# Reordering the first microseconds of a retention + ELU kernel: second chunk ahead of the first weight decode, powers later, one tile split by tokens

## The chip, the cores and the metric

The kernel runs on one core of one Trainium2 chip. The metric is the device time of that core in microseconds, over one launch. An engine name stands for the core's units: PE (matrix multiplication), DVE (vector), ACT (activation functions), POOL (general purpose), SP (which issues the transfers).

## What is computed

```python
# q, k, v: (4 batches, 8 heads, 768 positions, 64)
state = gamma * state + k_t^T v_t          # per head, 64 x 64
y_t   = (q_t . state) / sqrt(64)           # for every position t
x = y, heads side by side                  # (3072 tokens, 512)
h = x @ w_in                               # (512, 2048)
g = where(h > 0, h, exp(min(h, 0)) - 1)    # ELU
out = g @ w_out                            # (2048, 512)
```

`gamma` is one constant per head. All inputs and outputs are fp32; the weights arrive as 64-bit floats, of which the kernel itself makes fp32 numbers ("decode").

## The kernel before

**Tiling.** The 3072 tokens are handled in six blocks of 512; a block is four chunks of 128 tokens. One transfer of 1 MB (`load`, line 99) brings a chunk's q, k (turned) and k, v (plain). The retention is computed by chunk: powers of gamma are put on v (`scale_v`, line 275, which makes v'), a score matrix k q^T is masked (`score_products` 302, `mask_pair` 324), the state is k^T v' summed over half chunks of 64 tokens (`state_products` 332, `state_sum` 343), and the outputs are the masked part plus the part through the state (`within` 389, `across` 399), multiplied by powers of gamma out of a table `etab` (`powers_of`, line 246, four ACT exponentials per call). The result is the activations `xb`. The feed-forward part of the first block uses plain matrix products; the later blocks use Strassen's scheme on top of stored sums of weights. The change touches only the first block.

**Weights.** They come in 16 pieces of 1 MB (`load_piece`, line 126), of 64-bit words, into a ring of three staging buffers (`wraw`). `prepare` (line 147) issues the ACT part of a decode: two or three activations per part (lines 164, 166, 168). `decode` (line 180) is a generator with the DVE part: for each part a shift and mask (line 191, with a multiplication at line 190 ahead of it if `by_vector`), and an addition (line 194), after which the fp32 weights (`w_a`, `w_b`) are there. When the last part is done it also issues the load of the next piece. `take()` (line 1096) advances the generator by one step. Pieces 0, 1 and 2 are decoded in two halves of 512 columns.

**Order.** Nothing is scheduled automatically here. Each engine works through its instructions in the order in which the program text issues them, and lines 1106 to 1169 are a hand-written interleaving for the first 128 to 512 tokens. Generators hand out the work in steps:

- `outputs_of_first` (line 414) makes the activations of chunks 0 and 1 in two PSUM banks, `pb` and `pd`. Between the two groups of products into one bank stands a small DVE copy `seen` (line 426), for which the PE waits; line 433 writes `xb`.
- `plain_first` (line 489) makes 16 tiles of h, each of 128 rows of the result. The first five are begun on the first 256 tokens (`half[0]`, chunks 0 and 1), the rest of their tokens follows later. Tile 0 is further split: its first 128 tokens (chunk 0), a `yield`, then the next 128. Tiles 0 and 1 need the two halves of piece 0 (`w_a`), tiles 2 and 3 those of piece 1 (`w_b`), tile 4 the first half of piece 2. Tiles 0 to 4 are in the buffers pa, pa, pb, pd and hp.
- `unread` (line 1102) issues products of zeros whose result nobody reads.

In the order before, the first half of piece 0 is decoded on the DVE ahead of chunk 1's v' and mask, and the PE computes tile 0 on chunk 0 between chunk 1's scores and its k^T v'. The powers for tokens 256 to 767 (`between=` of `prepare`, line 1126) stand on the ACT between the two halves of piece 0. Chunks 2 and 3 are scaled by the POOL (line 281 as well, `scale_v(2)`, `scale_v(3)`); `scores(0, 1)` and `states(0, 1)` (lines 312 and 352) are their scores and states, `outputs(0, 1)` (line 364) their outputs, which read the later powers at line 384.

Of the kernel before, what the change touches and what calls it, by code (L numbers as in the profile page):

```python
# [18 lines left out]
def kernel(  # L19
# [36 lines left out]
    B, H, S, D, DM, DFF = dims  # L56
    NTOK = B * S
    C = P
    TB = 512
    TH = TB // 2  # L60
# [69 lines left out]
    def load_piece_parts(parts, behind=None):  # L130
        n = len(staged)
        if n < NPIECE:

            t = stage.tile([P, 1024, 2], U32, name="wraw", tag="stage")
            hold(t[:, :, 0].bitcast(FP32), behind)
            staged.append(t)
            for part in range(parts):
                if part:
                    yield
                c = slice(part * 1024 // parts, (part + 1) * 1024 // parts)  # L140
                d = slice(2 * c.start, 2 * c.stop)
                nc.sync.dma_start(t[:, c].rearrange("p c w -> p (c w)"), w_bits[n].bitcast(U32)[:, d])
# [1 line left out]

    def prepare(parts=1, by_vector=False, between=None):

        n = len(prepared)
        if n >= NPIECE:  # L150
            return
        t = staged[n]
        if n < 2 * NQ:
            dst = (w_a, w_b)[n % 2][n // 2].rearrange("p a b c d -> p (a b c d)")
        else:

            dst = w_s[n % NQ].rearrange("p a b c d -> p (a b c d)")[:, 0:1024]
        todo = []
        for part in range(parts):
            if part and between:  # L160
                between()
            c = slice(part * 1024 // parts, (part + 1) * 1024 // parts)
            lo, hi, flat = t[:, c, 0], t[:, c, 1], dst.bitcast(U32)[:, c]
            nc.scalar.activation(flat, lo, AF.Copy, scale=2.0**-29)
            top = dst.bitcast(F8).rearrange("p (c b) -> p c b", b=4)[:, c, 3]
            nc.scalar.activation(top, hi.bitcast(FP32), AF.Copy, scale=2.0**-120, saturate=False)
            if not by_vector:
                nc.scalar.activation(lo.bitcast(FP32), hi.bitcast(FP32), AF.Copy, scale=2.0**-112)
            todo.append((lo, flat, hi if by_vector else None))
        prepared.append((dst, todo))  # L170
# [9 lines left out]
    def decode(fine=False):  # L180

        n = len(decoded)
        if n >= NPIECE:
            return
        dst, todo = prepared[n]
        decoded.append(dst.rearrange("p (a b) -> p a b", a=2))
        vec = nc.vector
        for c, flat, hi in todo:
            if hi is not None:
                vec.tensor_scalar(c.bitcast(FP32), hi.bitcast(FP32), 2.0**-112, None, ALU.mult)  # L190
            vec.tensor_scalar(c, c, 3, 0x7FFFFFF8, ALU.logical_shift_left, ALU.bitwise_and)
            if fine:
                yield
            vec.tensor_tensor(out=flat, in0=c, in1=flat, op=ALU.add)
            yield
        load_piece()
        if n >= 2 * NQ:
            f = ORDER_F[n - 2 * NQ]
            nc.sync.dma_start(quarters(f)[:, used(f, 2, 8)], dst.rearrange("p (s c) -> p s c", c=P)[:, used(f, 2, 8)])
# [46 lines left out]
    def powers_of(tokens):  # L246
        for a in range(2):
            for u in range(2):
                nc.scalar.activation(etab[:, a, u, tokens], post[:, tokens], AF.Exp, scale=lny[:, a, u : u + 1])
# [4 lines left out]
    parts = load_piece_parts(2)  # L254
# [20 lines left out]
    def scale_v(m):  # L275
        if m >= NCHUNK:
            return
        i = chunks[m][1]
        qk, kv = raw[m]
        eng = nc.vector if m < 2 else nc.gpsimd  # L280
        eng.tensor_tensor(  # L281
            out=kv[:, 1], in0=kv[:, 1], in1=vf[:, i].unsqueeze(2).to_broadcast([C, H, D]), op=ALU.mult
        )
# [18 lines left out]
    def score_products(sc, tb, pp, x):  # L302
        qk = raw[tb * CPB + 2 * pp + x][0]
        for p in range(HP):
            for sub in range(2):
                for a in range(2):
                    nc.tensor.matmul(
                        sc[a][rows(sub), x, p, :], lhsT=qk[rows(a), 1, p, rows(sub)],
                        rhs=qk[rows(a), 0, p, rows(sub)], start=True, stop=True, skip_group_check=True,
                    )  # L310
# [32 lines left out]
    def state_sum(kvs, tb, pp, x, sub, copy=None):  # L343
        n = 4 * pp + 2 * x + sub
        if fresh(tb, n + 1):
            return
        if fresh(tb, n):
            (copy or nc.scalar.copy)(state(tb, n + 1), kvs[sub][:, x])
        else:
            nc.vector.tensor_tensor(out=state(tb, n + 1), in0=kvs[sub][:, x], in1=state(tb, n), op=ALU.add)  # L350
# [117 lines left out]
    def flush():  # L468
        while later:
            later.pop(0)()  # L470

    def elu(g, h, depth=1, then=None):


        r = epool.tile([P, 512], FP32, name="r", tag="r", bufs=3)
        e = r if len(h.shape) == 2 else r.rearrange("p (a c) -> p a c", c=P)
        nc.scalar.activation(e, h, AF.Relu, scale=-1.0)  # L477
        nc.scalar.activation(e, e, AF.Exp, scale=-1.0)  # L478

        def last():  # L480
            nc.vector.scalar_tensor_tensor(g, e, -1.0, h, ALU.add, ALU.max)  # L481
            if then:
                then()

        while len(later) >= depth:
            later.pop(0)()
        later.append(last)

    def plain_first():

        tiles = [(n, w, row, fi) for n in range(NQ) for w, row in ((w_a, 0), (w_b, 1)) for fi in range(2)]
        banks = []

        def part(k, columns):
            n, w, row, fi = tiles[k]
            for j in range(4):
                nc.tensor.matmul(
                    banks[k][:, columns], lhsT=w[n][:, fi, j // 2, j % 2, :], rhs=xb[:, j, columns],
                    start=(j == 0), stop=(j == 3), skip_group_check=True,
                )  # L500

        for k in range(5):
            hp = bank("aabd"[k]) if k < 4 else ps_r.tile([P, 2, TH], FP32, name="hp", tag="r")
            banks.append(hp.rearrange("p a b -> p (a b)"))
            if k == 0:
                part(0, slice(0, C))
                yield
                part(0, slice(C, 2 * C))
            else:
                part(k, half[0])  # L510
            if k:
                yield
        for k in range(5):
            part(k, half[1])
            n, w, row, fi = tiles[k]
            elu(g_plain[row * NF + 2 * n + fi], banks[k])
            yield
        for k, (n, w, row, fi) in enumerate(tiles[5:]):
            hp = bank("aabd"[k % 4]).rearrange("p a b -> p (a b)")
            for j in range(4):  # L520
                nc.tensor.matmul(  # L521
                    hp, lhsT=w[n][:, fi, j // 2, j % 2, :], rhs=xb[:, j, :], start=(j == 0), stop=(j == 3)
                )
            elu(g_plain[row * NF + 2 * n + fi], hp)
            yield
        flush()
# [158 lines left out]
    def bank(x):  # L685
        return ps_f.tile([P, 2, TH], FP32, name="p" + x, tag=x, bufs=2 if x == "a" else 1)
# [409 lines left out]
    def take(count=1):  # L1096
        for _ in range(count):
            next(piece, None)
# [3 lines left out]
    def unread(count, n):  # L1102
        for _ in range(count):
            nc.tensor.matmul(warm[:, 0:n], lhsT=blank[:, 0:P], rhs=blank[:, 0:n], start=True, stop=True, skip_group_check=True)
# [15 lines left out]
    y = outputs_of_first()  # L1120
    next(y)
    next(y)
    unread(1, TB)
    score_products(sc, 0, 0, 1)
    state_sum(kvs, 0, 0, 0, 1)
    prepare(2, between=lambda: powers_of(slice(2 * C, S)))
    piece = decode(True)
    take()
    take()
    scale_v(1)  # L1130
    mask_pair(sc, 1)
    inner = plain_first()
    next(inner)
    state_products(kvs, 0, 0, 1, range(2))
    state_sum(kvs, 0, 0, 1, 0)
    next(y)
    next(y)
    next(y)
    unread(1, TB)
    next(y, None)  # L1140
    take()
    take()
# [2 lines left out]
    scale_v(2)  # L1145
    scale_v(3)
    prepare(2, by_vector=True)
    next(inner)
    piece = decode()
    take()  # L1150
    take()
    next(inner)
    scores(0, 1)
    states(0, 1)
# [30 lines left out]
    for n, _ in enumerate(inner):  # L1185
# [8 lines left out]
        elif n == 10:  # L1194
            scores(1, 0)
            scores(1, 1)
            parts = sums_of_pieces(0)
# [21 lines left out]
    for n in second_of_first():  # L1219
        send_small()  # L1220
        if n == 0:
            run(inputs_of_first(4, [xslot(x) for x in range(3)]))
            parts = sums_of_pieces(2)
# [8 lines left out]
        elif n == 2:  # L1232
            next_piece()
            parts = sums_of_pieces(4)
# [5 lines left out]
        elif n == 4:  # L1240
            run(inputs_of_first(6, [hslot(), hslot(), xslot(0)]))
            decode_all()
            parts = sums_of_pieces(6)
# [85 lines left out]
    for tb in range(2, NTB):  # L1329
# [24 lines left out]
        tail, parts = iter(()), combine_x_parts()  # L1354
# [122 lines left out]
```

## Time and profile before

| what | value |
|---|---|
| median of 4 runs | 639.34 us (635.54, 640.03, 639.98, 638.70) |
| the profiled execution's own time | 635.54 us |
| its span, from the first to the last instruction | 633.7 us |
| PE busy | 626.1 us (99%) |
| DVE busy | 482.8 us (76%) |
| ACT busy | 253.4 us (40%) |
| POOL busy | 40.5 us (6%) |
| granted PE clock | 1.00 |

The profiled execution took 1.8 us more than its span, and is the fastest of the four. A busy PE counts every matmul from its start to a modelled end, so 99% doesn't mean that the PE has nothing left to gain, but its idle time is small. An fp32 matmul leaves two records in the trace: "x8" at line 497 is one tile's four matmuls. In the timeline, consecutive instructions of one kind are merged; the columns are the start, the time until the last one's end, the engine, the line, the operation, out<-in, the shapes, and in brackets the idle time before it with what ended it. Start times count from the start of the span. The addition at line 194 appears as CUSTOM_DVE_ANT_0.

### The profile page before, as it was taken

To read this page: it belongs to the slowest core of one execution; us is meant where nothing else is said; L and a number is where in the kernel's file an instruction comes from. 1 tells how busy PE (TensorE), PEld (TensorE's weight loads), DVE (VectorE), ACT (ScalarE), POOL (GpSimd) and SP (SyncE) were. 2 spreads that over 40 slices of the span, in tenths; PEclk is the share of its full clock that TensorE was granted. 3 is DMA by queue.
4 is the path that set the end of the run, shared out by engine and by line. 5 is a ranking of instruction groups with operands and counts; after the bars stand their busy time and mean duration, and the time that the engine had idled before them with its cause. 6 is when DMAs were issued, how large, how long until landed. Compare 5 with 4: busy or idle time off the path is not lost.

```text
span 633.7 us, 16149 instructions
## 1 busy us (share of the span) xinstructions
PE 626.1 (99%) x6680; PEld 560.5 (88%) x6680; DVE 482.8 (76%) x870; ACT 253.4 (40%) x472; POOL 40.5 (6%) x40
## 2 busy tenths in 40 slices
PE   8999999999999999999999999999999999999998
PEld 5764578888899999889999989999988999988997
DVE  5779979978879675589676588767489878558975
ACT  6599636014551113554112546111465311366311
POOL 1121000003600000200000100000110000000000
PEclk9999999999999999999999999999999999999999
DMA  8798868687477788504989701889820798700794
GB/s 337 269 399 315 252 202 234 189 250 258 176 230 241 242 258 274 220 2 139 287 259 314 285 2 54 258 284 287 302 100 5 219 300 259 216 20 2 229 310 159
DMA packets 75897, 136.85 MB, mean 216 GB/s; under 512 B 6320, under 2 KB 31792, under 8 KB 70704
## 3 DMA queue, kind: packets, MB, share of 16 engines
q1 hardware_dynamic: 75824, 135.82, 65.1%
q8 instruction: 53, 0.87, 0.5%
q14 instruction: 20, 0.16, 0.1%
HBM read 114.56 MB, written 21.23 MB: 214 GB/s over the span
## 4 chain that ended last, share of the span: by engine, by line
PE 93%; DVE 4%; DMA 1%; issue 1%; ACT 0%; SPq 0%; DVEq 0%
PE pa L953 20%; PE pa L911 10%; PE pd L953 10%; PE pb L953 5%; PE pa L865 5%; PE pb L911 4%; PE pa L521 3%; PE qa L911 3%; PE x L611 3%; PE pa L740 2%; PE pd L865 2%; PE qd L911 2%; PE pd L911 2%; PE pa L611 2%; PE y L394 2%; PE kv L338 2%
## 5 line engine op out<-in xcount | busy, mean ns | idle before, releaser
L961 ACT COPY ms<-pa 128x128 f32<-128x128 f32 x104 | 27.7, 267 | 147.0 <-PE pa L953 143.5
L953 PE MATMUL pa<-ts,wq 128*128 128x128 f32 x560 | 74.2, 275 | 0.0
L953 PE MATMUL pd<-ts,wq 128*128 128x128 f32 x552 | 73.6, 276 | 0.1
L953 PEld LDWEIGHTS pa<-ts,wq 128*128 128x128 f32 x560 | 68.5, 192 | 0.4
L953 PEld LDWEIGHTS pd<-ts,wq 128*128 128x128 f32 x552 | 67.1, 192 | 0.9 <-DVE res L965 0.5
L953 PE MATMUL pa<-gC,wq 128*128 128x128 f32 x480 | 64.6, 278 | 0.0
L478 ACT ACTIVATE r<-r 128x512 f32<-128x512 f32 x96 | 60.7, 632 | 3.0
L953 PEld LDWEIGHTS pa<-gC,wq 128*128 128x128 f32 x480 | 59.0, 192 | 1.3
L477 ACT ACTIVATE r<-gC 128x512 f32<-128x512 f32 x64 | 40.0, 625 | 33.0 <-DVE gC L919 33.0
L965 DVE TENSOR_TENSOR res<-pd,ms 128x128 f32<-128x128 f32 x68 | 19.5, 287 | 39.6 <-PE pd L953 38.4
L281 POOL TENSOR_TENSOR chunk<-chunk,vf 128x512 f32<-128x512 f32 x22 | 26.3, 1198 | 319.0 <-DMA chunk<-in_qkv_dram 235.1
L481 DVE SCALAR_TENSOR_TENSOR gC<-r,gC 128x512 f32<-128x512 f32 x64 | 45.3, 740 | 0.7 <-ACT r L478 0.7
L827 DVE TENSOR_TENSOR ts<-gC,ts 128x512 f32<-128x512 f32 x60 | 41.3, 688 | 1.0
L827 DVE TENSOR_TENSOR ts<-gC 128x512 f32<-128x512 f32 x60 | 41.0, 684 | 0.0
L953 PE MATMUL pb<-gC,wq 128*128 128x128 f32 x240 | 31.7, 275 | 0.0
L986 ACT COPY res<-pa 128x128 f32<-128x128 f32 x34 | 9.1, 267 | 55.0 <-PE pa L953 55.0
L953 PEld LDWEIGHTS pb<-gC,wq 128*128 128x128 f32 x240 | 29.2, 192 | 0.0
L690 ACT COPY m<-pa 128x512 f32<-128x512 f32 x24 | 14.0, 581 | 29.0 <-PE pa L911 13.2
L919 DVE TENSOR_TENSOR gC<-qa,gC 128x512 f32<-128x512 f32 x8 | 5.5, 692 | 25.1 <-PE qa L911 18.3
L911 PE MATMUL pa<-xt,w_s 128*128 128x256 f32 x96 | 23.0, 382 | 0.0
L911 PE MATMUL pa<-xt,w_b 128*128 128x256 f32 x96 | 23.0, 382 | 0.0
L965 DVE TENSOR_TENSOR res<-res 128x512 f32<-128x512 f32 (+1 forms) x31 | 20.6, 666 | 3.0 <-DVE res L965 0.5
(256 smaller groups left out, 1258.0 us busy)
## 6 DMA issues: line engine op xcount, KB each, us to landing
wq<-scratch_dram SPq DMA_DIRECT2D x277, 256.0 KB, 4.3
chunk<-in_qkv_dram SPq DMA_DIRECT2D x23, 1024.0 KB, 8.2
wraw<-in_w_dram SPq DMA_DIRECT2D x15, 1024.0 KB, 6.1
out_dram<-res SPq DMA_DIRECT2D x14, 256.0 KB, 3.8
scratch_dram<-gT SPq DMA_DIRECT2D x12, 256.0 KB, 4.1
scratch_dram<-m SPq DMA_DIRECT2D x12, 192.0 KB, 5.7
scratch_dram<-so SPq DMA_DIRECT2D x4, 512.0 KB, 4.8
scratch_dram<-wi SPq DMA_DIRECT2D x2, 1024.0 KB, 5.1
```

The source lines that it names most:

```text
L281: eng.tensor_tensor(out=kv[:, 1], in0=kv[:, 1], in1=vf[:, i].unsqueeze(2).to_broadcast([C, H, D]), op=ALU.mult)
L477: nc.scalar.activation(e, h, AF.Relu, scale=-1.0)
L478: nc.scalar.activation(e, e, AF.Exp, scale=-1.0)
L481: nc.vector.scalar_tensor_tensor(g, e, -1.0, h, ALU.add, ALU.max)
L521: nc.tensor.matmul(hp, lhsT=w[n][:, fi, j // 2, j % 2, :], rhs=xb[:, j, :], start=(j == 0), stop=(j == 3))
L611: nc.tensor.matmul(X[j][:, d, :], lhsT=w[j][:, d * P : d * P + P], rhs=x[j], start=(n == 0 and d == 0), stop=at_end, skip_group_check=True,)
L827: sub = lambda o, x, y: nc.vector.tensor_tensor(out=o, in0=x, in1=y, op=ALU.subtract)
L865: nc.tensor.matmul(ps[:, f, :], lhsT=lhs[f], rhs=xs[j][k], start=(begin and f == 0), stop=True, skip_group_check=True,)
L911: nc.tensor.matmul(ps[:, fi, :], lhsT=w[:, fi, j2, :], rhs=x[:, j2, :], start=(j in (1, 7) and fi == 0 and j2 == 0), stop=(j2 == 1), skip_ ...
L953: nc.tensor.matmul(ps, lhsT=w[:, f, :], rhs=ts[j][k][:, f, :], start=(begin and f == 0), stop=(f == 3), skip_group_check=True,)
L961: nc.scalar.copy(m, ps)
L965: nc.vector.tensor_tensor(out=o, in0=x, in1=y, op=ALU.add)
```

## The change

Only the order of instructions in the first block changes, with one tile split and two products of zeros shortened or dropped. The second call `unread(1, TB)` of this part shrinks to 256 columns and the third is dropped. The first piece's two DVE steps go behind chunk 1's v', mask and state sum, one on each side of the `seen` copies. Tile 0 on chunk 0 goes behind all of chunk 1's outputs on the PE. The four exponentials for the later tokens go behind the ACT part of piece 1. Tile 3 on the first 256 tokens is split into two halves of 128 tokens: one ahead of the scores of chunks 2 and 3, one behind their k^T v'. Queues of SP and POOL keep their order.

```diff
-    def prepare(parts=1, by_vector=False, between=None):
+    def prepare(parts=1, by_vector=False):
...
-            if part and between:
-                between()
...
+            elif k == 3:
+                part(k, slice(0, C))
+                yield
+                part(k, slice(C, 2 * C))
             else:
                 part(k, half[0])
...
     y = outputs_of_first()
     next(y)
     next(y)
-    unread(1, TB)
+    unread(1, TH)
     score_products(sc, 0, 0, 1)
     state_sum(kvs, 0, 0, 0, 1)
-    prepare(2, between=lambda: powers_of(slice(2 * C, S)))
+    prepare(2)
     piece = decode(True)
-    take()
-    take()
     scale_v(1)
     mask_pair(sc, 1)
-    inner = plain_first()
-    next(inner)
     state_products(kvs, 0, 0, 1, range(2))
     state_sum(kvs, 0, 0, 1, 0)
     next(y)
+    take()
     next(y)
+    take()
     next(y)
-    unread(1, TB)
+    inner = plain_first()
+    next(inner)
     next(y, None)
     take()
     take()
...
     scale_v(2)
     scale_v(3)
     prepare(2, by_vector=True)
+    powers_of(slice(2 * C, S))
     next(inner)
     piece = decode()
     take()
     take()
+    next(inner)
     next(inner)
     scores(0, 1)
     states(0, 1)
```

## Prediction, made before the changed kernel ran

> **What bounds the kernel now.** I read the page's busy rows first, then the PE's waits, then the timelines of PE, DVE, POOL and ACT from 8 to 32 us, where every edit lies, and last the chain of work that ended last.
>
> ```profile
> span 633.7 us, 16149 instructions
> PE 626.1 (99%) x6680; PEld 560.5 (88%) x6680; DVE 482.8 (76%) x870; ACT 253.4 (40%) x472; POOL 40.5 (6%) x40
> ```
>
> ```profile
> 10.38 0.69 PE L307 MATMUL sc<-chunk 64*64 64x64 f32 x32
> 11.32 1.13 PE L497 MATMUL pa<-xb,w_a 128*128 128x128 f32 x8 [0.25 <-DVE w_a L194]
> 12.38 0.69 PE L338 MATMUL kv<-chunk 64*64 64x64 f32 x32
> ...
> 14.69 1.12 PE L1104 MATMUL pa<-blank 128*128 128x512 f32 x2
> 15.65 3.11 PE L497 MATMUL pa<-xb,w_a 128*128 128x128 f32 x16
> 19.28 1.99 PE L497 MATMUL pb<-xb,w_b 128*128 128x256 f32 x8 [0.52 <-DVE w_b L194]
> 21.21 1.16 PE L307 MATMUL sc<-chunk 64*64 64x64 f32 x64
> ...
> 28.05 1.97 PE L497 MATMUL hp<-xb,w_a 128*128 128x256 f32 x8
> ```
>
> The PE is the bound: 633.7 - 626.1 = 7.6 us of it are idle in the whole span, and even with useless products counted as idle the stretch of the change has only a few us to give. After tile 4 (hp, 28.05) the chain that ended last runs through the PE without a gap to 46 us; DMA holds 1% of it in all, its first 4.9 us. So a shift of tile 4's start should be carried to the end: what I predict is that start.
>
> ```profile
> 10.48 0.69 DVE L194 CUSTOM_DVE_ANT_0 w_a<-wraw,w_a 128x1024 uint16<-128x1024 uint16 x1
> 11.09 0.69 DVE L281 TENSOR_TENSOR chunk<-chunk,vf 128x512 f32<-128x512 f32 x1
> 11.69 0.75 DVE L328 TENSOR_TENSOR chunk<-sc,cmask 128x256 f32<-128x256 f32 x2
> ...
> 17.92 1.31 DVE L194 CUSTOM_DVE_ANT_0 w_b<-wraw,w_b 128x1024 uint16<-128x1024 uint16 x1
> ...
> 20.17 1.35 DVE L194 CUSTOM_DVE_ANT_0 w_b<-wraw,w_b 128x1024 uint16<-128x1024 uint16 x1
> ```
>
> ```profile
> 17.51 1.17 POOL L281 TENSOR_TENSOR chunk<-chunk,vf 128x512 f32<-128x512 f32 x1 [2.39 <-DMA chunk<-in_qkv_dram]
> 19.93 1.04 POOL L281 TENSOR_TENSOR chunk<-chunk,vf 128x512 f32<-128x512 f32 x1 [1.25 <-DMA chunk<-in_qkv_dram]
> ```
>
> ```profile
> 9.69 2.55 ACT L249 ACTIVATE etab<-so,lny 128x512 f32<-128x512 f32 x4
> 12.42 0.69 ACT L164 ACTIVATE w_a<-wraw 128x512 uint32<-128x512 uint32 x1 [0.19 <-DMA wraw<-in_w_dram]
> ...
> 22.44 0.69 ACT L164 ACTIVATE w_a<-wraw 128x512 uint32<-128x512 uint32 x1 [4.67 <-DMA wraw<-in_w_dram]
> ```
>
> See three things. Chunk 1's scores start at 10.38, when its transfer is there, but its v' waits on the DVE behind the decode until 11.09. The same addition takes 0.69 us for `w_a` and 1.31 and 1.35 us for `w_b`, where POOL's scaling runs; both times it ends 0.55 us after POOL does (18.68 to 19.23, 20.97 to 21.52). And the ACT waits for transfers, on both sides of the powers.
>
> **The parts and their cost.**
>
> *Powers behind piece 1.* Four activations, 2.55 us, moved. Piece 0's second half still can't start before its transfer at 12.42 (0.19 us of wait today), so nothing is gained on the ACT. Piece 1's ACT part ends at 17.77 (16.98 + 0.79), the powers then run to 20.3, inside the 4.67 us wait before 22.44; their reader, the write of the second half of `xb`, comes at 28.12. Cost nothing, cover 2.1 us; were it gone, piece 2 and tile 4 would wait for it.
>
> *Products of zeros.* The halved one starts at 9.23 and is followed by the wait for chunk 1: no gain. The dropped one gives back 15.65 - 14.69 = 0.96 us, but only if `xb` and `w_a` are there earlier.
>
> *Chunk 1 first.* v' starts with its transfer at about 10.4 instead of 11.09 and ends at 11.05; the masks end at about 11.85 (12.44 before); k^T v' starts at 11.1, not 12.38, as tile 0's 0.9 us (the spacing of four 128-column matmuls in the later stages) no longer stands ahead of it. The state sum (13.11 before) runs 11.83 to 12.26, the PE's first products through it end at about 12.7. The moved shift (0.42 us) fits in between, 12.2 to 12.6, on the DVE ahead of `seen`, for which the PE waits: it costs nothing there by 0.1 us, and up to 0.1 if late. `seen` comes at 12.72 against 14.00: 1.28 us gained. The moved addition (0.69) follows, 12.9 to 13.6. Behind it on the DVE stand the two writes of `xb`: 13.5 to 14.25 (15.58 before); the PE's chunk 1 products are done by 13.5 and tile 0 waits for this addition till 13.65.
>
> *Tiles 0, 1, 2.* Tile 0's halves: 13.65 to 14.55 and, `xb` being there, to 15.45. Piece 0's second half on the DVE: shift at 14.5 (ACT ends at 14.44), addition to 15.65 (16.65 before). Tile 1: 15.7 to 17.45 (1.73 us, as four 256-column matmuls in the chain from 33 us on). Piece 1's first half: state sum 15.55, multiplication 15.9, shift 16.35, addition 16.9 to 17.6, just ahead of POOL's start at 17.51, hence 0.69 and not 1.31 us. Tile 2: 17.65 to 19.4, against 19.28: 1.63 us ahead.
>
> *Piece 1's second half against POOL.* [...] POOL's start is set by chunk 2's transfer and stays at about 17.5, [...] one of multiplication, shift and second addition is held for about 1 us: the addition ends at 20.2. By the rows without a block (0.42 + 0.43 + 0.69 and 0.2 of gaps) it would be 19.4; before it is 21.52. I take 20.2, as both collisions in the trace were lost by the DVE. So the block moves rather than goes.
>
> *Tile 3 split.* The same columns, four more matmuls and weight loads. Loads take 0.19 us and overlap; the later stages run 128-column matmuls in 0.9 us per four, against 1.73 / 2 = 0.87. Cost 0 to 0.1 us, taken as 0. Its first half waits for the addition: 20.25 to 21.15. The new wait is on the PE, and everything behind it (scores of chunks 2 and 3, their states) stands 0.06 us ahead of before. The second half saves 0.87 us behind the states: scores to 22.15, states to 23.15, tile 3's rest to 24.05, chunk 2 and 3's outputs from there (25.16 before).
>
> *To tile 4.* Outputs: 1.2 us of masked products, then those through the states, done by 25.75 (27.05). The DVE's masks and sums (22.35 to 25.4) are hardly earlier than before; its last sums, the shift and `seen` end at 26.0 without the 1.2 us of idle that they have before. DVE and PE now meet here. Second products through the states: 26.05 to 26.75, the addition for tile 4 done at about 26.7. Tile 4: 26.75 instead of 28.05.
>
> Sum: 1.28 us at `seen`, 1.63 at tile 2, 0.06 at the scores, 1.3 at tile 4: **1.3 us less**. Loads of pieces 3 and 4 are issued about 1 us earlier on SP, into queues that are full until 26 us: nothing. The profiled execution would go from 635.54 to 634.2. The other runs lie 3 to 4.5 us above it; taken off the median: 639.34 - 1.3 = **638.0 us**.
>
> **The rivals.**
>
> [...] (0.15). Its instructions are issued back to back, and POOL could wait until the second addition. Tile 3 then starts at 19.45, all behind it 0.8 us earlier: 2.1 us, 637.2. [...] Against: POOL was served each time before.
>
> *The DVE takes all* (0.18). If POOL's two instructions block twice (multiplication at 17.5, addition at 19.93), masks, sums and `seen` come 1 us later, tile 4 at 27.75: 0.3 us, 639.0; a second small delay, or `seen` behind a late shift, and it is no change. For it: the DVE has no idle left to absorb.
>
> *The clock falls* (0.12): slower. The products of zeros keep the PE busy. A 512-column one took 1.14 us at 1.5 us and 0.64 us at 9 to 15 us, though the granted clock shows 1.00 for both. [...] My longest new gap is 0.9 us (19.4 to 20.25)[...].
>
> **How the numbers follow.** The likeliest case has 0.55. A difference of 0.5% (3.2 us) is about what a measurement of this kernel can tell from no change, and no case reaches it: all waits and zeros of the stretch that can be recovered are under 3 us. What lies outside comes from the runs' scatter (635.5 to 640.0) [...]: faster 0.11, slower 0.07, within 0.82. The range goes from 635.3 (2.1 us gained, and the median halfway towards the fastest run) to 640.4 (the slow rival).
>
> **What would show it.** v' of chunk 1 on the DVE at 10.4; the first addition at 12.9; tile 0 at 13.65; `w_b` additions of about 0.7 us, first at 16.9, with a POOL or DVE instruction stretched by up to 1 us at 17.5; tile 3's first half at 20.25; tile 4 at 26.75, and the same shift in each later stage. I am wrong if tile 4 starts later than 27.7, if matmuls from 13.65 to 20 take twice their time, or if the 1.3 us are there at 28 us and gone at the end.

## The result, and the profile after

The change makes the kernel a little slower. The medians of all runs are 638.94 us after (636.67 to 641.98, 43 runs) and 637.01 us before (635.14 to 640.51, 64 runs; the median of the four runs shown ahead of the prediction was on the high side). The ratio is 1.0026, 95% interval 1.0017 to 1.0034: about 1.7 us (0.0026 x 637) more, where 1.3 us less had been forecast. The profiled execution after took 638.62 us, 2.0 us of it outside its span.

The page's first rows. PE busy falls by 0.9 us while the span grows by 2.9 us, so this is not more work but more idle time:

```profile
span 636.6 us, 16163 instructions
PE 625.2 (98%) x6686; PEld 560.6 (88%) x6686; DVE 481.1 (76%) x870; ACT 253.3 (40%) x472; POOL 40.4 (6%) x40
```

The PE's waits in the whole span (what it waited for, us in total, times, longest). The kernel before has no row with the releaser "issue", which is idle time for which the profile finds no semaphore:

```profile
PE y L407 <- issue: 1.3, 2, 0.9
PE pd L495 <- issue: 0.8, 1, 0.8
...
PE kv L336 <- issue: 0.5, 1, 0.5
PE pd L495 <- DVE w_b L192: 0.4, 1, 0.4
...
PE pb L955 <- issue: 0.2, 1, 0.2
```

The PE's timeline shows where they lie. Line numbers are now two lower around the retention, so L495, L305, L336, L407 answer to L497, L307, L338, L409:

```profile
10.41 0.69 PE L305 MATMUL sc<-chunk 64*64 64x64 f32 x32 [0.51 <-DMA chunk<-in_qkv_dram]
11.14 0.50 PE L336 MATMUL kv<-chunk 64*64 64x64 f32 x17
12.10 0.40 PE L336 MATMUL kv<-chunk 64*64 64x64 f32 x12 [0.46 <-issue]
...
14.46 3.77 PE L495 MATMUL pa<-xb,w_a 128*128 128x128 f32 x24 [0.23 <-ACT wraw L166]
18.23 1.97 PE L495 MATMUL pb<-xb,w_b 128*128 128x256 f32 x8
20.63 1.16 PE L495 MATMUL pd<-xb,w_b 128*128 128x128 f32 x8 [0.43 <-DVE w_b L192]
21.71 1.16 PE L305 MATMUL sc<-chunk 64*64 64x64 f32 x64
...
23.74 1.05 PE L495 MATMUL pd<-xb,w_b 128*128 128x128 f32 x7
25.61 0.27 PE L495 MATMUL pd<-xb,w_b 128*128 128x128 f32 x1 [0.82 <-issue]
...
27.77 0.69 PE L407 MATMUL y<-chunk 64*64 64x64 f32 x31 [0.33 <-DVE seen L376]
29.34 0.21 PE L407 MATMUL y<-chunk 64*64 64x64 f32 x1 [0.89 <-issue]
29.48 1.99 PE L495 MATMUL hp<-xb,w_a 128*128 128x256 f32 x8
```

Each stop falls in the middle of a run of equal matmuls: after 17 of 32 records, after 7 of 8, and after 31 of 32, just ahead of tile 4. The profile names no data for which the PE waits there. Tile 4 starts at 29.48 us, 1.43 us later than before and 2.73 us later than predicted.

### The profile page after: what moved, and what is told of

Its sections match the earlier page's. It is cut to its first block, busy times and chain, and to the rows that moved or that the text cites. A ratio compares the mean times of both kernels' runs of the same rounds, so it can differ in the third digit from the quotient of the medians.

```text
span 636.6 us, 16163 instructions
## 1 busy us (share of the span) xinstructions
PE 625.2 (98%) x6686; PEld 560.6 (88%) x6686; DVE 481.1 (76%) x870; ACT 253.3 (40%) x472; POOL 40.4 (6%) x40
## 4 chain that ended last, share of the span: by engine, by line
PE 87%; DVE 6%; DMA 2%; ACT 2%; issue 2%; SPq 0%; DVEq 0%
PE pa L955 20%; PE pa L913 10%; PE pd L955 10%; PE pb L955 5%; PE pa L867 5%; PE pb L913 4%; PE qa L913 3%; PE x L613 3%; PE pa L742 2%; PE pd L867 2%; PE qd L913 2%; PE pa L613 2%; PE pd L913 2%; PE y L392 2%; PE y L407 2%
## 5 line engine op out<-in xcount | busy, mean ns | idle before, releaser
L913 PE MATMUL pa<-xb,w_a 128*128 128x256 f32 x96 | 22.7, 379 | 0.0
```

The source lines that it names most:

```text
L913: nc.tensor.matmul(ps[:, fi, :], lhsT=w[:, fi, j2, :], rhs=x[:, j2, :], start=(j in (1, 7) and fi == 0 and j2 == 0), stop=(j2 == 1), skip_ ...
```

## What stops the PE

I counted the PE's records in the trace (weight loads, matmuls and its other instructions, in order of time): 13,614 before, 13,627 after. The instructions themselves come by DMA, in packets of 16 KB, as the page's part 3 shows (packets, MB, share of the engines):

```profile
q8 instruction: 53, 0.87, 0.5%
```

53 x 256 is 13,568, which fits 256 instructions to a packet. All the stops lie at records 193 + 256 k of the stream ("block ends" below): 449, 961 and 1217 early in the kernel after, 4801 and 6593 later. At these five stops the packet of the block that the PE needs starts 1.1 to 5.5 us after the PE has crossed the block end before it, takes about 1 us, and the PE goes on 1.36 to 1.45 us after the packet has ended. The 13 profiles of this document have 676 block ends: at none does the PE go on sooner than 1.18 us after its packet has ended, also where it doesn't stop. So at stops like these the PE goes on about 3.5 us (1.1 + 1 + 1.4) or more after it entered the block before; that is an estimate from these figures. Blocks of long matmuls last longer, and the packets are there in time: the 12 blocks of the kernel after that hold no product of the retention lasted 13.5 to 29.5 us, and the packet needed at the end of each had ended 8.0 us or more before the PE went on there. A block of the retention's 64x64 products need not last as long: 64 matmul records with their 64 loads take about 1 us (1.16 us at 21.71), at least half of the 256 records ahead of each stop are of that kind, and those blocks lasted 2.6 to 7.1 us.

With the change the block end 449 falls into chunk 1's k^T v', which now starts at 11.14, ahead of the block; before, it started at 12.38, when the block was there. The end 1217 lay 11 instructions inside tile 4, where it left a gap of 0.2 us; now it lies in the outputs just ahead of tile 4. In the kernel before, one stop is above 0.25 us (0.27 us at 77 us); after, there are five, 3.99 us in sum, of which 2.87 us (0.67 + 1.10 + 1.10) come before tile 4. The last two are 2.20 of the 2.73 us by which tile 4 misses the prediction; 0.38 more had been lost when tile 3's first half started (20.63 instead of 20.25). The stop at 449 doesn't add in full, as part of it went into the wait for `w_b` there.

The tile's split adds 16 instructions (four more matmuls and four loads, each of which leaves two records in fp32); the dropped product of zeros takes 4 away, and there is one more semaphore: +13.

Theory A, **instruction blocks**: the loss is stops at block ends, made by the count of instructions ahead of the dense stretches and by their earlier start. Theory B, **the moves**: the new order itself costs, for example by the powers behind piece 1, DVE against POOL, or later weight loads; the count doesn't matter. A third, the **clock** (the prediction's rival), is taken up where the traces show it.

## The experiments

Ratios are to the kernel before, with 95% intervals (6 executions each for the two with +48, 10 to 22 for the others, 43 for `after`). "Stops" are those over 0.25 us at block ends in the one profiled execution, counted as above; a wait of 0.96 us at end 705 of `after_p48` is left out, as its packet had been there for 3.4 us and the PE waited for `w_b`. The products of zeros in the opening loop (`range(28)`) serve as a dial: four of them are 16 instructions, their result is read by nobody, and no computed work is changed.

| kernel | edit | ratio | stops, sum in us | tile 4 at, us |
|---|---|---|---|---|
| before | | 1 | 1, 0.27 | 28.05 |
| after | the change | 1.0026 [1.0017, 1.0034] | 5, 3.99 | 29.48 |
| after_m16 | after, 28 to 24 | 1.0033 [1.0018, 1.0048] | 2, 2.55 | 30.05 |
| before_p16 | before, 28 to 32 | 1.0024 [1.0003, 1.0044] | 6, 3.85 | 29.72 |
| after_p48 | after, 28 to 41, one `unread` less | 1.0072 [1.0052, 1.0092] | 2, 2.98 | 30.10 |
| before_p48 | before, the same | 1.0080 [1.0057, 1.0102] | 3, 3.75 | 29.98 |
| after_nosplit | after, tile 3 whole | 0.9995 [0.9977, 1.0014] | 0, 0.00 | 29.36 |
| after_nosplit_p16 | the same, 28 to 32 | 1.0021 [1.0013, 1.0030] | 3, 2.40 | 28.88 |
| before_split | before, tile 3 split | 1.0038 [1.0024, 1.0052] | 5, 3.39 | 30.22 |
| after_powers_back | after, powers as before | 1.0025 [1.0013, 1.0038] | 5, 3.65 | 29.23 |
| after_nosplit_again | as after_nosplit | 0.9993 [0.9977, 1.0009] | 2, 1.33 | 27.41 |
| before_m16 | before, 28 to 24 | 1.0028 [1.0014, 1.0043] | 3, 2.18 | 28.47 |
| after_nosplit_m8 | after_nosplit, 28 to 26 | 1.0014 [1.0000, 1.0028] | 3, 1.55 | 27.39 |

The stops are not all that a profile lost. In four of the profiles the granted clock falls to 0.50 for 3.41 us: `after_nosplit` (from 12.31 us), `after_m16` (15.10), `after_p48` (12.52 and 227.56) and `before_p48` (229.22). Each of these five stretches begins 0.4 to 1.8 us after the end of an idle time of 1.45 to 1.90 us, at a stop or in a wait for chunk 1. (Idle means that neither a matmul nor a weight load is on record.) The other idle times between the first scores and the last matmul are at most 1.13 us long, and none is followed by such a stretch.

### The count alone, up and down

The kernel before with four more products (`before_p16`); `after_m16` has 24 in the same line of the kernel after.

```diff
-    for n in range(28):
+    for n in range(32):
```

> The kernel before, with 32 instead of 28 small products of zeros at the start: 16 more PE instructions, nothing else moved. Theory (PE instruction blocks): the block's end, 11 instructions into tile 4 today, falls 4 instructions ahead of it, so tile 4 waits for the fetch: it starts at 29.0 to 29.2 instead of 28.05 us and the kernel is about 1.0 us slower (ratio 1.0016), without any part of the change. Rivals (DVE and POOL, clock): at most the 0.2 us that the four products take, and those are in a wait for the first transfer: ratio 1.0000.

> The changed kernel with 24 instead of 28 small products of zeros at the start: 16 fewer PE instructions ahead of everything, nothing else moved. Theory (PE instruction blocks): in the changed kernel the PE stops at instruction 193 + 256k of its own stream (449, 961, 1217) until 1.4 us after the instruction transfer of that block has ended; the last such stop (1.1 us) stands right before tile 4. With 16 fewer instructions the block's end falls 14 instructions into tile 4, whose matmuls are slow enough to hide the fetch: tile 4 starts at about 28.3 instead of 29.48 us, and the time is 1.2 us below the changed kernel, about 0.5 us above the kernel before. Rival ([...] the multiplication held 1.27 us at 18 us): no vector instruction moves, so no change, tile 4 at 29.4, 1.7 us above the kernel before. Rival (clock, fewer zeros): if anything slower.

`before_p16` moves nothing and adds four tiny products, and is slower by 0.24%. The PE's timeline has the stops of the kernel after at the same places:

```profile
25.74 0.70 PE L497 MATMUL pd<-xb,w_b 128*128 128x256 f32 x2 [0.43 <-issue]
...
28.32 0.69 PE L409 MATMUL y<-chunk 64*64 64x64 f32 x30 [0.33 <-DVE seen L378]
29.47 0.33 PE L409 MATMUL y<-chunk 64*64 64x64 f32 x2 [0.45 <-issue]
29.72 1.56 PE L497 MATMUL hp<-xb,w_a 128*128 128x256 f32 x6
```

Two stops before tile 4 (0.81 and 0.67 us) and four later ones make the 3.85 us of the table. (In this profile chunk 1's scores also started 0.7 us later than before, at 11.08; see "Open".) B can't explain that. But `after_m16` didn't win the time back. The stop at 1217 is gone, as expected, and a longer one has come at 449, where the packet ran 10.95 to 11.91 us (9.79 to 10.68 in the kernel after):

```profile
11.20 0.62 PE L336 MATMUL kv<-chunk 64*64 64x64 f32 x25
13.27 0.28 PE L336 MATMUL kv<-chunk 64*64 64x64 f32 x4 [1.45 <-issue]
...
15.52 5.18 PE L495 MATMUL pa<-xb,w_a 128*128 128x128 f32 x24 [0.17 <-DVE w_a L192]
```

The last row is tiles 0 and 1, which took 3.77 us in the kernel after: from 15.10 to 18.51 us the clock was at half. So the count sets where the ends lie, but not simply how much is lost: a slightly later end (the one at 193 was crossed at 7.18 us instead of 6.92) gave a packet 1.2 us later, and behind the long stop the clock fell, which cost 1.41 us more. Without these 1.41 us tile 4 would have stood at about 28.6 us (30.05 - 1.41, an estimate), near the 28.3 expected. The clock isn't the whole of the miss in the times, though: the 10 executions of `after_m16` at a clock of 0.999 or more still have a median of 637.9 us, against 636.3 for those of the kernel before.

### Forty-eight more

```diff
-    for n in range(28):
+    for n in range(41):
...
     mask_pair(sc, 0)
-    unread(1, TH)
```

> The changed kernel with 41 instead of 28 small products of zeros at the start and without the 256-column one behind chunk 0's scores: 48 more PE instructions ahead of chunk 0's products of v. Theory (PE instruction blocks): block ends fall into chunk 1's scores (reached later than the fetch lands), into tile 2, into chunk 3's states (23.4 us) and into the last products through the states; only the last one still stops the PE, by under 1 us, at about 27.1. Tile 4 at 27.1 to 27.6 us, about 2 us below the changed kernel and 0.5 to 0.9 us below the kernel before, which is what the prediction had counted on. Rivals (DVE and POOL, clock): as the changed kernel, 1.7 us above the kernel before, tile 4 at 29.4.

> The kernel before with the same 48 PE instructions more at the start: a control, which says whether such instructions are of use by themselves. Theory (PE instruction blocks): only one stop of 0.2 us at 25.3 us is there to be removed, tile 4 at 27.8 to 28.1 us, ratio 0.9995 to 1.0005. Rival (the zeros help by the clock): the gain of the other kernel with 48 would show here as well, 2 us.

Missed in both. I had worked out the early ends only. In both kernels the end 4801 now falls into the outputs at 227 us, with the same long stop; the first line is of the kernel before with this edit, the second of the kernel after with it:

```profile
227.60 0.34 PE L409 MATMUL y<-chunk 64*64 64x64 f32 x7 [1.84 <-issue]
```

```profile
227.15 0.46 PE L407 MATMUL y<-chunk 64*64 64x64 f32 x14 [1.85 <-issue]
```

That two orders share it speaks for A: the place follows the count. The stop at 4801 (2.07 us after, 2.06 before) and the later tile 4 (2.05 and 1.93 us) make about 4 of the 4.6 and 5.1 us lost. Right behind this stop the clock is at half for 3.41 us in both; the clock row of the page of `before_p48`, 16 us to a digit, shows it as the one 8:

```profile
PEclk9999999999999989999999999999999999999999
```

Chunk 1's scores also started 0.9 to 1.0 us later here (11.35 and 11.30); that part is not settled, see "Open".

### The split alone, and the change without it

```diff
-            elif k == 3:
-                part(k, slice(0, C))
-                yield
-                part(k, slice(C, 2 * C))
...
-    next(inner)
     scores(0, 1)
```

`before_split` adds these lines to the kernel before, and moves nothing else; `after_nosplit` takes them out of the kernel after.

> The kernel before with tile 3 split by tokens as in the change, and nothing else: 16 more PE instructions ahead of tile 4. Theory (PE instruction blocks): as with 16 products' worth of instructions at the start, a stop of about 1 us ahead of tile 4, which starts at 29 to 29.7 instead of 28.05 us, plus the wait of tile 3's first half for its weights at 21.5 us; 1 to 2 us slower (ratio 1.0015 to 1.003). Rival (the split is free and saves PE time ahead of the outputs): 0 to 0.9 us faster.

> The changed kernel with tile 3 left whole, behind the states of chunks 2 and 3, as before. Theory (PE instruction blocks): 16 fewer instructions stand ahead of tile 4, so the block's end falls into tile 4 instead of right ahead of it, and the scores, no longer behind tile 3's wait for its weights, start when chunk 3 has landed (20.2 to 20.5 us instead of 21.7), which also starts the next fetches earlier. Tile 4 at 26.8 to 27.6 us instead of 29.48; 1.5 to 2.5 us below the changed kernel, 0 to 1 us below the kernel before (ratio 0.998 to 1.000). The stop at instruction 449 (chunk 1's states, 12 us) stays. Rival (the loss comes from the moves in the first 16 us, not from the split): as the changed kernel, ratio 1.0026. Rival (DVE held by POOL): the second half of piece 1 is late as before, but nothing waits for it ahead of 22 us, so it can't be told from the first.

> The same with 32 instead of 28 small products of zeros: 16 more PE instructions, so the block's end stands two instructions ahead of tile 4 again, as in the changed kernel. Theory (PE instruction blocks): a stop right ahead of tile 4, of about 1 us: tile 4 at 28 to 28.5 us, 0.8 to 1.3 us slower than without these products. Rival (only the order of PE, DVE and ACT matters): the same time as without them.

The split alone costs 0.38%; the rest of the change, without the split, shows no cost (0.9995, and 0.9993 when it was run again). `after_nosplit_p16` has no split but as many PE records as the kernel after (13,627), and is slow again, 1.0021. So most of the split's price is its instructions, not its order. In the first profile of `after_nosplit` chunk 1's scores started only at 11.89 us and the clock was at half behind that wait, so its tile 4 at 29.36 says little.

> The changed kernel without the split of tile 3 once more: for a narrower interval, and for a profile with another landing of chunk 1's transfer, which came 1.5 us late in the first one. Theory (PE instruction blocks): ratio 0.998 to 1.000 as before; if chunk 1 lands at 10.4 us, tile 4 at 26.8 to 27.6 us, with a stop of about 0.6 us at instruction 449 and none at 961 and 1217. If the moves of the first 16 us were themselves the loss, tile 4 would stand at 28.05 us or later with chunk 1 at 10.4.

The second profile of the change without the split, in which chunk 1 landed as early as in the kernel after, gives the account. The PE's timeline:

```profile
18.22 1.97 PE L495 MATMUL pb<-xb,w_b 128*128 128x256 f32 x8
20.11 1.16 PE L305 MATMUL sc<-chunk 64*64 64x64 f32 x64
...
24.88 1.05 PE L392 MATMUL y<-chunk 64*64 64x64 f32 x57 [0.48 <-issue]
...
26.72 0.69 PE L407 MATMUL y<-chunk 64*64 64x64 f32 x32 [0.33 <-DVE seen L376]
27.41 1.97 PE L495 MATMUL hp<-xb,w_a 128*128 128x256 f32 x8
```

Tile 2 starts at the same time as in the kernel after (18.22, 18.23), tile 4 2.07 us earlier. Without the split the scores follow tile 2 at once, at 20.11. With it, tile 3's first half stands there and waits for `w_b` until 20.63: 0.52 us. The remaining ends cost 1.10 + 1.10 with the split and 0.69 (at 961) without: 1.51 us. 0.52 + 1.51 = 2.03 of the 2.07 us. The times agree, within wide intervals: 1.0026 - 0.9993 is 0.0033, 2.1 us. The multiplication beside POOL's scaling takes as long in this kernel, 1.27 us, and `w_b` comes at the same time (20.55 and 20.57 us); so DVE against POOL shows no cost by itself, only through the wait that the split puts ahead of the scores.

### The powers, and two more counts

> The changed kernel with the four exponentials back between the two halves of piece 0, where they stood before. All theories: they stand in a wait of the ACT in either place, so no change from the changed kernel, ratio to before 1.002 to 1.003. If they had been the cause, the ratio would go to 1.000.

```diff
-    prepare(2)
+    prepare(2, between=lambda: powers_of(slice(2 * C, S)))
...
-    powers_of(slice(2 * C, S))
```

1.0025 against 1.0026: the move of the powers shows no cost, as predicted. B has lost its first candidate.

Two more counts: the kernel before with 24 products (`before_m16`), and `after_nosplit` with 26 in the same line (`after_nosplit_m8`).

```diff
-    for n in range(28):
+    for n in range(24):
```

> The kernel before with 24 instead of 28 small products of zeros: 16 fewer PE instructions, the counterpart of 16 more. Theory (PE instruction blocks): the block's end moves from tile 4 into the tile behind it, so no stop ahead of tile 4; at most one of 0.6 us at instruction 449, if its fetch comes late: ratio 0.9995 to 1.001, against 1.0024 with 16 more. Rival (any change in the number of these products disturbs the start): slower by as much as with 16 more.

> The changed kernel without the split and with 26 instead of 28 small products of zeros: a try at a version that beats both, as the first block's end is crossed a little later, [...]. Theory (PE instruction blocks): no stop ahead of tile 4, ratio 0.997 to 1.000. Other theories: as without the split.

`before_m16` was expected at no change and is slower, 1.0028. Tile 4 is only 0.4 us later, 0.57 of stop being at 449; a longer stop stands at 1729, in the second block of tokens:

```profile
65.25 0.85 PE L338 MATMUL kv<-chunk 64*64 64x64 f32 x37
67.12 0.39 PE L338 MATMUL kv<-chunk 64*64 64x64 f32 x6 [1.01 <-issue]
```

I had again thought of the early ends only; the stops of 2.18 us in sum do fit the 1.8 us. `after_nosplit_m8` lies between `after_nosplit` and the slow ones, with 1.55 us of stops. Over the table, every kernel with over 2 us of stops is slower than before, the one with 1.55 has an interval that just touches no change, and the two that aren't slower have 0 and 1.33. It isn't a straight line: the two with +48 lose more than their stops, and `after_m16` with 2.55 loses as much as `after` with 3.99. These three are kernels in whose profiles the clock fell behind a stop.

## Why the prediction was wrong, step by step

**Right.** Chunk 1's v' started at 10.39 (10.4 predicted). The powers hid where they should, on the ACT with 2.54 us of wait left behind them:

```profile
17.60 2.54 ACT L247 ACTIVATE etab<-so,lny 128x512 f32<-128x512 f32 x4
22.67 0.69 ACT L162 ACTIVATE w_a<-wraw 128x512 uint32<-128x512 uint32 x1 [2.54 <-DMA wraw<-in_w_dram]
```

Beside POOL's first scaling it is now another DVE instruction that takes longer, as the step on piece 1's second half had it. DVE and POOL timelines:

```profile
17.39 0.69 DVE L192 CUSTOM_DVE_ANT_0 w_b<-wraw,w_b 128x1024 uint16<-128x1024 uint16 x1
18.00 1.27 DVE L188 TENSOR_SCALAR wraw<-wraw 128x512 f32<-128x512 f32 x1
...
19.87 0.70 DVE L192 CUSTOM_DVE_ANT_0 w_b<-wraw,w_b 128x1024 uint16<-128x1024 uint16 x1
```

```profile
17.91 1.07 POOL L279 TENSOR_TENSOR chunk<-chunk,vf 128x512 f32<-128x512 f32 x1 [2.86 <-DMA chunk<-in_qkv_dram]
```

The first addition now takes 0.69 us; the multiplication behind it, 0.42 us elsewhere, takes 1.27 and ends 0.29 us after POOL (18.98). In the profile before, no multiplication ran beside POOL's scaling, so that a multiplication takes longer there shows only here. The second addition ended at 20.57 instead of 20.2; POOL's scaling ended 0.3 us later than before.

**The rival of the clock.** Tile 2's four 256-column matmuls take 1.97 us, against 1.99 before, and the granted clock stayed at 1.00 in the profile after: the rival of a falling clock isn't what made tile 4 late there. It isn't out for the times. A clock below 0.999 over the whole execution stands in 60 of the 174 executions on record of the eight kernels with the change (9 of 44 of `after`), and in 18 of the 195 recorded with a clock of those without it. For `after` that is a small part: leaving the nine out lowers its median by 0.3 us. The idle times that were followed by half the clock were 1.45 to 1.90 us long; the longest new gap of the prediction was 0.9 us.

**Wrong, first: "Tile 3 split. ... Cost 0 to 0.1 us, taken as 0."** This is the term that turned the sign. I priced four more matmuls by their time on the array, which came out nearly as priced (1.08 and 0.97 us for the halves, 1.93 for the whole tile before), and put nothing for their 16 instructions, which move every later block end. What they cost: 1.51 us at tile 4 in the profiles, and 0.0027 of the time (1.0021 against 0.9994, the mean of the two), or 1.7 us, by the count alone.

**Wrong, second: the new wait was compared with the wrong kernel.** I noted that everything behind tile 3's first half stands "0.06 us ahead of before". Against the same change without the split it stood behind a wait of 0.52 us in which the scores could have run, and my own numbers had that wait in them (tile 2 to 19.4, the half from 20.25).

**Wrong, third: "k^T v' starts at 11.1" and the state sum at 11.83.** It started at 11.14, but stopped after its 17th record for 0.67 us; the sum came at 12.58, `seen` at 13.47 instead of 12.72. The 1.28 us of gain there became 0.53.

The upper end of the range, 640.4 for the slow rival, was my estimate and rests on no trace.

**What became of the rest.** Later in the kernel the ends 4801 and 6593 cost 0.52 and 0.60 us. In the profiled execution 0.7 us more were lost at about 72 us, where the outputs of the second block wait for a DVE sum, behind a weight piece that landed late (the ACT waited 1.30 us for it at 55 us, before not at all). The kernel's loads there are the same. Six of the eight profiles with the change have this wait of the PE (0.3 to 0.6 us), and one of the five without, so it may belong to the change; no run tests it. Without the split the change should still have given up to 1.3 us. It gave 0.64 at tile 4 and 1.0 us of span in one profile, and 0.3 to 0.5 us in the times, with intervals that include no change. Part of the rest is the clock: among executions at 0.999 or more its medians are 635.8 and 635.7 us, against 636.4 and 636.5 of the kernel before, 0.6 and 0.8 us less. Its two stops, 0.64 and 0.69 us, are the likeliest place of the remainder, which is not shown; no count that was tried removes both and adds none.

**Open.** Chunk 1's transfer lands at 10.3 to 10.6 us in most profiles and at 11.1 to 11.9 in five. In four of the five the first block end was crossed about 1 us earlier, so that an instruction packet was fetched ahead of part of that chunk; in the fifth, `after_nosplit`, it wasn't. That a packet delays the chunk is therefore only a guess. It doesn't set the verdicts alone: `after_m16`, `before_split` and `before_m16` are slow, and their profiles have an early chunk 1. Why the clock fell more often with the change is open too: the shortened product of zeros stood ahead of the wait for chunk 1, and the stops are new idle time, but no run separates them.

## What to carry to other kernels

An instruction can have a price even where its execution is hidden (here 0.0027 of the time for 16 of them): on an engine that is never idle, count the instructions, find where the ends of the instruction blocks fall, and see whether a stretch of short instructions stands there. A stop marked "issue" in the middle of a run of equal matmuls (0.43 to 1.85 us here) was the sign of it. For a gain of some tenths of a per cent, first move the count alone in the kernel before (a few useless products, at no other change) and see how much the time scatters with it; here that was 0.2 to 0.3% for four products (0.8% with 48 instructions more), more than the whole expected gain. Price each part of a change against the change without that part, not only against the kernel before. And where a profile has a long pause (here 1.45 us or more), read the clock behind it as well.

## What the runs showed of the hardware

The arrival of instructions stopped the PE. In the kernel after, each of the 52 packets ended 1.36 us or more before the PE went on into the block that the count gives it, and began while an earlier block ran. At 36 of the 52 ends the PE shows no gap above 0.05 us; at the five stops 150 to 255 of the 256 records ahead are of 64x64 products, and the gaps are 0.52 to 1.10 us, 3.99 us in sum. The longest of all profiles is 2.07 us, in `after_p48`. The time from crossing an end to the start of the next packet varies: 1.1 us for the packet at 27 us (the DMA engines were 10% busy from 26.24 to 27.90), but 1.3 us for that at 23 us and 2.9 us for that at 10 us, where they were fully busy (share 1.04 from 22.60 to 24.20, 1.00 from 9.30 to 10.70), and 5.5 us at the end 6593. Nine of the 52 packets of the kernel after began 0.2 to 3.6 us before the PE's records reached the end before. What sets this time is not shown.

A short pause of the PE was followed by half its clock: between the first scores and the last matmul of the 13 profiles, all five idle times of 1.45 to 1.90 us were, for 3.41 us each, and none of those of up to 1.13 us was. That the pause is the cause is argued from this and not tested.
